# A fused attention, gated layer and SoLU layer on one core: the last pair's end on GpSimd, four raw buffers, new tables of due times and dummy transposes

## The chip, the cores and the metric

The kernel runs on one core of a Trainium2 chip. The metric is the device time of one execution in microseconds (us). The core's engines work side by side, each through its own queue in order: TensorE (PE, matmuls and transposes), VectorE (DVE), ScalarE (ACT), GpSimd (POOL) and SyncE (SP, which here only issues DMAs). They wait for one another by semaphores.

## The reference

Three layers in a row, all in float32 with 64-bit weights (float64 in the inputs):

```python
# 1. attention: 4 batches, 8 heads, 576 tokens, 64 per head, q and k rotated
scores = 1 / sqrt(64) * rotate(q) @ rotate(k).T
attn = exp(scores - max(scores)); attn /= sum(attn) + 1e-9
x = (attn @ v) -> [2304 tokens, 512]
# 2. gated layer, 512 -> 1536 -> 512
x = (sigmoid(x @ w_gate) * (x @ w_val)) @ w_out
# 3. SoLU layer, 512 -> 1024 -> 512
h = x @ w_in; s = h * softmax(h)
out = (((s - mean) / sqrt(var + 1e-6)) * g_ln) @ w_out
```

## The kernel before, in words

**Precision.** Each float32 operand of a matmul is split into a high part in float32r (an ACT or DVE copy) and a low part (a subtraction on DVE or POOL), and three products are added. So around every matmul there are copies and subtractions on the other engines.

**Attention** runs 16 pairs of heads (`i`, `NPR` = 16; pair `i` is batch `i // 4`, heads `2 * (i % 4)` and the next). A pair has nine score tiles (`order`, `NTL` = 9). For each tile PE makes the scores (`scores`), DVE the row maximum, ACT the exponentials, PE four transposes of them (`transpose_e`, "te"), ACT and DVE the two halves of the transposed tile ("et"), and PE the products with v (`attend`, "av"). POOL rotates q and k of the next pair (`turn`), and PE, ACT and DVE turn those into the stacked operands (`qk_bank`, "bank"). For the first pair this is done by hand: `turn_first` rotates in four parts on DVE and POOL, `qk_bank(0, part)` transposes into three PSUM banks, and 20 small copies and subtractions (`job_first`, `stack_first`, named `first.head.step.n`) fill the operands; the scores of head 0 need those of head 0. At a pair's end two joins (DMA) bring the halves of two heads together, two adds and one scale write x in SBUF (`add`, `scale_x`: on POOL, for the last pair on DVE), and `x_out` writes x to memory, from SP. Around the end of this layer the first unit of the gated layer is already computed (`plain`), from x of the first blocks (`x_plain`), and the first weights are decoded (`job_early`).

**Order in attention.** Every step is a job with an engine, what it reads and writes, and a due time from the table `NEED`: a key such as `te.5.2` (step te, tile 5, third job) gives a time, to which 16.83 us (`PERIOD`) times the pair is added; `@0`, `@15` override it for one pair. `emit_attention` sorts the jobs by due time and each engine gets its own in that order. The times that jobs carry there (`took`) and `gate` do not enter it.

**The gated layer** runs three groups of weights (`s`) over three blocks of 768 tokens (`b`), each with four units of products (7 products by Strassen's scheme, only the very first block plainly) and two outputs. The weights come as 64-bit words: SP loads a raw tile, ACT makes the magnitude (`w_mag`, into `mag`), DVE joins sign, magnitude and low bits (`w_sign`, `w_or_mag`, `w_or_low`); this is `decode`, and it has two raw and two magnitude buffers in turn. `split_x` splits x of a block, `keep_p` and `keep_i` decode the weights of the third layer in between and put them by in memory. `KEEP_I` says from which time of which block.

**The SoLU layer** runs nine pairs of token tiles (`job_h`, `job_n`, `job_p`, `job_u`, `job_j`).

**Order in the later layers.** `run_jobs` plans them: a list scheduler with assumed durations that gives each engine, when it is free, the ready job with the lowest due time. Here the due times are written in the code, as `need - 5` and the like. SP's queue holds first the DMAs of attention and then those of this plan.

The change touches `qk_bank` (212), `x_out` (363), the first banks (669), `job_scores` (723), `turned_out` (742), `job_add` (783), `job_scale` (804), `job_x_out` (809), `NEED` (1027), `decode` (1204) and `KEEP_I` (1316).

Of the kernel before, what the change touches and what calls it, by code (L numbers as in the profile page):

```python
# [20 lines left out]
def kernel(  # L21
# [21 lines left out]
    nc = tc.nc  # L43
# [168 lines left out]
    def qk_bank(i, part):  # L212

        raw = turned[i].rearrange("p i h d -> p i (h d)")
        if part == 0:
            stacks[i, 0] = st_t[i % 2][0]
            stacks[i, 1] = st_t[i % 2][1]
# [145 lines left out]
    def x_out(hp, bl, c, n):  # L363
        nc.sync.dma_start(out=xd[bl][hp, :, c - bl * BT:c - bl * BT + n], in_=x_sb[hp][:, c:c + n])
# [284 lines left out]
    if True:  # L649
# [72 lines left out]

    def job_scores(g):
        i, n = divmod(g, NTL)
        begin("scores", i, n)
        reads = []
        for h in (0, 1) if order[n] is None else (order[n][0],):
            reads += row_stacks(i, h, 0, 3)
        if order[n] is None:
            reads.append(one(f"qtl{i % 2}", 0, 2))  # L730
        took = (1.06 if order[n] is None else 0.53) * (2.0 if g < 4 else 1.0)
        writes = [one(f"S{g % 2}")] + ([one(f"sum{i % 4}", 0, NTL)] if n == 0 else [])
        ajob(nc.tensor, took, lambda: found.__setitem__(("s", g), scores(i, n)), reads, writes)
# [33 lines left out]
    def job_attend(i, h, j, m0, m1):  # L767
# [4 lines left out]
        if m1 == 9:  # L772
            e = (A, V)[SLOTS["uw"][2 * h + j]]
            ajob(e, 0.365 if e is V else 0.3, lambda: high(e, *found["av"][0][1:]), (one("AV"),), (one(uw, *c),))
# [8 lines left out]
    def job_add(i, h):  # L783
        e = (G, V)[i == NPR - 1]
        ajob(e, 1.42 if e is G else 0.67, lambda: add(i, h, e), (one(f"uw{(2 * i + h) % 4}", 0, S), one(f"um{i % 2}", h, h + 1)), (x_rows(i, h),), True)
# [10 lines left out]
    def job_weigh_out(i):  # L796
        ajob(V, 0.2, lambda: weigh_out(i, 0), (found.pop(("tr", i)),), (one("rt"),))
# [6 lines left out]
    def job_scale(i):  # L804
        e = (G, V)[i == NPR - 1]
        x = [x_rows(i, h) for h in range(2)]
        ajob(e, 1.42 if e is G else 0.67, lambda: scale_x(i, e), [one(f"wt{i % 2}", 0, 3)] + x, x, True)

    def job_x_out(i):
        b, hp = pairs[i]  # L810
        c = b * S
        while c < (b + 1) * S:
            bl = c // BT
            n = min((bl + 1) * BT, (b + 1) * S) - c
            ajob(SP, n * 0.5 * KB, lambda bl=bl, c=c, n=n: x_out(hp, bl, c, n), [x_rows(i, h) for h in range(2)], (one(f"xd{bl}", hp, hp + 1),))
# [34 lines left out]
    def job_stack_left(i):  # L850
        for h in range(2):
            ajob(G, 0.2, lambda h=h: stack_left(i, h), row_stacks(i, h, 1, 2, "l"), (one(f"qtl{i % 2}", h, h + 1),))
# [107 lines left out]
    for m, t in enumerate((7.9, 10.0, 10.25)):  # L960
# [60 lines left out]
    for m in chunks:  # L1021
# [939 lines left out]
```

## Time and profile before

| | |
|---|---|
| median of 3 runs | 915.3 us (914.73 to 915.69) |
| profiled execution | 915.11 us, its span 913.2 us |
| busy, share of the span | PE 97%, DVE 89%, ACT 72%, POOL 37% |
| TensorE's mean granted clock | 0.997 of full |
| DMA | 147.33 MB, mean 161 GB/s |

The span runs from the first to the last instruction of the profiled execution. A busy time is the time in which an engine had an instruction at work; matmuls overlap, and their ends are modelled. A line number is that of the kernel. A releaser is what ended an engine's wait.

### The profile page before, as it was taken

To read this page: it belongs to the slowest core of one execution; us is meant where nothing else is said; L and a number is where in the kernel's file an instruction comes from. 1 tells how busy PE (TensorE), PEld (TensorE's weight loads), DVE (VectorE), ACT (ScalarE), POOL (GpSimd) and SP (SyncE) were. 2 spreads that over 40 slices of the span, in tenths; PEclk is the share of its full clock that TensorE was granted. 3 is DMA by queue.
4 is the path that set the end of the run, shared out by engine and by line. 5 is a ranking of instruction groups with operands and counts; after the bars stand their busy time and mean duration, and the time that the engine had idled before them with its cause. 6 is when DMAs were issued, how large, how long until landed. Compare 5 with 4: busy or idle time off the path is not lost.

```text
span 913.2 us, 16106 instructions
## 1 busy us (share of the span) xinstructions
PE 882.9 (97%) x5354; PEld 833.1 (91%) x5354; DVE 810.2 (89%) x1523; ACT 653.5 (72%) x1379; POOL 339.3 (37%) x296
## 2 busy tenths in 40 slices
PE   4999999999999999999999999999999999999998
PEld 3999999999998999999999999999999877888886
DVE  5999999999997798999998999999987499999971
ACT  4999999999995465666667666666565276777751
POOL 7679899898845000011011121212030243233200
PEclk9999999999999999999999999999999999999999
DMA  4667777678663762425275864659599834454332
GB/s 127 159 183 196 205 200 197 184 209 214 155 165 112 221 216 81 151 81 196 86 230 135 260 133 145 129 174 229 179 250 364 185 124 93 99 109 81 81 70 46
DMA packets 120882, 147.33 MB, mean 161 GB/s; under 512 B 44752, under 2 KB 90080, under 8 KB 120800
## 3 DMA queue, kind: packets, MB, share of 16 engines
q1 hardware_dynamic: 113888, 136.87, 51.4%
q0 software_dynamic: 6912, 9.44, 7.1%
q8 instruction: 42, 0.69, 0.3%
q14 instruction: 40, 0.33, 0.1%
HBM read 77.76 MB, written 37.30 MB: 126 GB/s over the span
## 4 chain that ended last, share of the span: by engine, by line
PE 73%; DVE 19%; issue 3%; DMA 2%; ACT 2%; POOL 0%; SPq 0%; DVEq 0%; ACTq 0%
PE s L291 9%; PE av L420 8%; PE te L379 7%; DVE xs L544 2%; PE tq L222 2%; PE far_c L1869 2%; PE far_b L1869 2%; PE far_c L1871 2%; PE far_b L1870 2%; PE far_c L1870 2%; PE far_b L1871 2%; PE tk L400 1%; DVE w L469 1%; PE near_a L630 1%; PE near_a L629 1%
## 5 line engine op out<-in xcount | busy, mean ns | idle before, releaser
L298 DVE TENSOR_REDUCE nm<-s 128x1 f32<-128x576 f32 x144 | 108.2, 752 | 11.5 <-PE s L291 9.0
L303 ACT ACTIVATE e<-s,nm 128x576 f32<-128x576 f32 x144 | 107.7, 748 | 7.4 <-DVE nm L298 6.0
L291 PE MATMUL s<-st 128*128 128x288 f32 x512 | 96.6, 312 | 5.5 <-DVE st L251 3.9
L373 DVE TENSOR_TENSOR et<-te,et 128x512 fp32r<-128x512 f32 x144 | 95.8, 676 | 1.4 <-ACT et L370 1.3
L420 PE MATMUL av<-et,vs 128*128 128x288 f32 x512 | 94.4, 312 | 0.4 <-POOL vs L202 0.4
L1457 POOL DMA_DIRECT2D yd<-yst x40 | 36.0, 1280 | 141.1 <-ACT yst L486 141.1
L370 ACT CAST et<-te 128x512 fp32r<-128x512 f32 x144 | 81.2, 587 | 7.8 <-PE te L379 6.4
L379 PE MATMUL te<-ident,e 128*128 128x128 f32 x576 | 81.9, 274 | 2.5 <-DVE et L373 2.4
L291 PEld LDWEIGHTS s<-st 128*128 128x128 f32 x512 | 75.1, 193 | 6.8 <-ACT st L249 4.2
L420 PEld LDWEIGHTS av<-et,vs 128*128 128x128 f32 x512 | 73.3, 191 | 0.7 <-POOL vs L202 0.6
L379 PEld LDWEIGHTS te<-ident,e 128*128 128x128 f32 x576 | 67.4, 141 | 5.1 <-DVE et L373 2.5
L540 ACT CAST xs<-xst 128x384 fp32r<-128x384 f32 x110 | 50.7, 518 | 13.7 <-DVE xst L535 11.5
L544 DVE TENSOR_TENSOR xs<-xst,xs 128x384 fp32r<-128x384 f32 x112 | 56.4, 548 | 2.2 <-ACT xs L540 2.0
L1538 POOL TENSOR_TENSOR xs<-xst,xs 128x512 fp32r<-128x512 f32 (+1 forms) x14 | 17.5, 1254 | 72.7 <-ACT xs L1535 72.7
L431 POOL TENSOR_TENSOR x_sb<-uw,um 64x576 f32<-64x576 f32 x30 | 43.2, 1439 | 2.5 <-DMA um<-uw 0.4
L494 POOL TENSOR_TENSOR wv<-w,wv 128x512 fp32r<-128x512 f32 (+1 forms) x3 | 5.2, 1743 | 103.3 <-ACT wv L486 103.3
L170 POOL TENSOR_TENSOR turned_t<-raw_t,other_t 128x576 f32<-128x576 f32 (+1 forms) x30 | 40.5, 1369 | 1.2
L463 ACT ACTIVATE mag<-raw_w 128x512 f32<-128x512 f32 x52 | 34.9, 676 | 7.9 <-DMA raw_w<-in_moe_w_val_dram 3.7
L162 POOL TENSOR_TENSOR other_t<-raw_t,rope_sb 128x1152 f32<-128x1152 f32 x14 | 37.4, 2674 | 5.6 <-DMA raw_t<-in_q_dram 4.5
L162 POOL TENSOR_TENSOR raw_t<-raw_t,rope_sb 128x1152 f32<-128x1152 f32 x14 | 37.3, 2664 | 1.1
L1811 POOL TENSOR_TENSOR st<-st,mhalf 128x1 f32<-128x1 f32 x18 | 15.9, 884 | 54.9 <-DVE st L1810 53.7
L629 PE MATMUL near_a<-xs,wg 128*128 128x384 f32 x96 | 32.3, 337 | 2.1 <-ACT held L1363 2.1
(475 smaller groups left out, 3068.4 us busy)
## 6 DMA issues: line engine op xcount, KB each, us to landing
st<-st SPq DMA_DIRECT2D x45, 288.0 KB, 4.0
xst<-xd SPq DMA_DIRECT2D x32, 384.0 KB, 6.0
raw_w<-in_moe_w_out_dram SPq DMA_DIRECT2D x20, 512.0 KB, 4.5
yd<-yst POOLq DMA_DIRECT2D x40, 192.0 KB, 6.5
st<-st SPq DMA_DIRECT2D x47, 144.0 KB, 2.4
raw_w<-in_moe_w_gate_dram SPq DMA_DIRECT2D x12, 512.0 KB, 4.3
raw_w<-in_moe_w_val_dram SPq DMA_DIRECT2D x12, 512.0 KB, 3.7
cd<-mag SPq DMA_DIRECT2D x22, 256.0 KB, 5.5
```

What stands on the lines that cost most here:

```text
L162: eng.tensor_mul(out=(o, x)[step], in0=x, in1=w.to_broadcast([P, n, 2, D // 2]))
L291: nc.tensor.matmul(ps[:, j, :HALF], w, x, start=m == 0, stop=m == len(mm) - 1)
L298: nc.vector.tensor_reduce(out=nm, in_=ps[:, :, :HALF], axis=AX.XY, op=ALU.max, negate=True)
L303: nc.scalar.activation(out=e.rearrange("p (j c) -> p j c", j=2), in_=ps[:, :, :HALF], func=AF.Exp, bias=nm, accum_out=sums[i][:, n:n + 1],)
L370: nc.scalar.copy(out=h_out, in_=ps)
L373: nc.vector.tensor_sub(out=l_out, in0=ps, in1=h_out.bitcast(F32))
L379: nc.tensor.transpose(ps[:, r * P:(r + 1) * P], e[:, r * P:(r + 1) * P], ident)
L420: nc.tensor.matmul(av[:, :HALF], *mm[m], start=m == 0, stop=m == len(mm) - 1)
L431: eng.tensor_add(out=x_sb[hp][rows, b * S:(b + 1) * S], in0=uws.pop((i, h))[rows], in1=uws[i][rows])
L540: nc.scalar.copy(out=t[:, 0], in_=here)
L544: l_eng.tensor_sub(out=t[:, 1], in0=here, in1=t[:, 0].bitcast(F32))
L629: nc.tensor.matmul(out, wh, t[:, 0], start=fresh and j == 0, stop=False, skip_group_check=not fresh)
```

## The change

1. **The last pair's end.** `job_add` and `job_scale` use POOL for all pairs. The last pair's `x_out` is issued from POOL's queue; for the others it stays on SP.
2. **Raw buffers.** The first six decodes of the gated layer use four raw and four magnitude buffers in the order 0, 2, 3, 1, 0, 2 (magnitudes 0, 2, 3, 1, 0, 2); the two new ones of each kind lie in the tiles yst and xst, which have no other use yet.
3. **The attention table.** All 446 entries of `NEED` have new values (below, a few of them set together).
4. **Dummy transposes.** `keep_clock(n)` issues n transposes of the identity into a PSUM tile that nobody reads: 30 before the first banks, 16 behind them, and 5, 5 and 4 behind the scores of tiles 1, 2 and 3 of the first pair.
5. **Shifts.** In the later layers each job gets a name (`place`), and a table `SHIFT` of 800 entries adds a number of us to the due times of the jobs that it names. `KEEP_I` starts the two jobs 6 and 5 us earlier. Some assumed durations differ, of which only that of `w_sign` (0.34 to 0.36) reaches the planner of the later layers.

```diff
-    def x_out(hp, bl, c, n):
-        nc.sync.dma_start(out=xd[bl][hp, :, c - bl * BT:c - bl * BT + n], in_=x_sb[hp][:, c:c + n])
+    def x_out(hp, bl, c, n, eng):
+        eng.dma_start(out=xd[bl][hp, :, c - bl * BT:c - bl * BT + n], in_=x_sb[hp][:, c:c + n])
...
+        idle_ps = ps_av.tile([P, 512], F32, tag="av", name="idle")
+
+        def keep_clock(n):
+            for _ in range(n):
+                nc.tensor.transpose(idle_ps[:, 0:P], ident, ident)
+
+        keep_clock(30)
         first.extend(qk_bank(0, part)[0][2] for part in range(3))
-        pass
+        keep_clock(16)
...
+    IDLE_AFTER = {1: 5, 2: 5, 3: 4}
...
+        def run():
+            found["s", g] = scores(i, n)
+            if i == 0 and n in IDLE_AFTER:
+                keep_clock(IDLE_AFTER[n])
...
     def job_add(i, h):
-        e = (G, V)[i == NPR - 1]
-        ajob(e, 1.42 if e is G else 0.67, lambda: add(i, h, e), ...)
+        ajob(G, 1.42, lambda: add(i, h, G), ...)
...
     def job_scale(i):
-        e = (G, V)[i == NPR - 1]
...
+            e = (SP, G)[i == NPR - 1]
+            ajob(e, n * 0.5 * KB if e is SP else 1.3, lambda bl=bl, c=c, n=n, e=e: x_out(hp, bl, c, n, e), ...)
...
     NEED = {
-        "first.0.0.0": -33.81, "first.0.0.1": -62.21, "first.1.0.0": -47.43,
+        "first.0.0.0": -320.064, "first.0.0.1": -167.555, "first.1.0.0": -241.355,
...
-        "te.4.2@15": 32.63, "softmax.8.0@15": 35.64, "add.0.0@15": 65.1,
+        "te.4.2@15": 39.745, "softmax.8.0@15": 49.04, "add.0.0@15": 91.357,
...
-        "early.3.v.1.1536.3": 292.64, "early.3.v.1.1536.4": 294.63, "x_plain.B22.1.1": 262.71, "plain.7.0": 326.42,
+        "early.3.v.1.1536.3": 285.916, "early.3.v.1.1536.4": 288.006, "x_plain.B22.1.1": 380.509, "plain.7.0": 481.022,
...
+    plain_job, names_of = job, []
+    SHIFT = { ... }
+    def job(eng, took, fn, reads=(), writes=(), need=0.0, port=None):
+        key = f"{step[0]}.{step[2]}"
+        step[2] += 1
+        names_of.append(key)
+        plain_job(eng, took, fn, reads, writes, need + SHIFT.get(key, 0.0), port)
...
+    RAWS = [(raw_w[n], one(f"raw{n}")) for n in range(2)]
+    RAWS += [(yst_t[:, 1024 * n:1024 * n + 1024].bitcast(I64), one("yst", 1024 * n, 1024 * n + 1024)) for n in range(2)]
+    MAGS = [(mags[n], one(f"mag{n}")) for n in range(2)]
+    MAGS += [(xst_t[:, 2048 + 512 * n:2560 + 512 * n], one("xst", 2048 + 512 * n, 2560 + 512 * n)) for n in range(2)]
+    AHEAD = [(RAWS[r], MAGS[m]) for r, m in ((0, 0), (2, 2), (3, 3), (1, 1), (0, 0), (2, 2))]
...
-    KEEP_I = {(2, 0): (0, 36.0), (2, 1): (1, 25.0)}
+    KEEP_I = {(2, 0): (0, 30.0), (2, 1): (1, 20.0)}
```

## Rows read from the trace of the kernel before

**Rows 1.** The page's head and its part 1, busy us of each engine.

```profile
span 913.2 us, 16106 instructions
PE 882.9 (97%) x5354; PEld 833.1 (91%) x5354; DVE 810.2 (89%) x1523; ACT 653.5 (72%) x1379; POOL 339.3 (37%) x296
```

**Rows 2.** Stages: length; busy us (xinstructions) PE, PEld, DVE, ACT, POOL; PEclk; DMA; GB/s.

```profile
0.00:40.00 40.00, 25.80 (x157) 23.16 (x158) 28.83 (x59) 26.69 (x63) 25.23 (x26) 1.00 0.53 137
16.00:26.00 10.00, 9.25 (x48) 8.87 (x47) 5.83 (x10) 6.29 (x16) 9.84 (x8) 1.00 0.42 109
40.00:60.00 20.00, 20.00 (x161) 19.31 (x160) 19.10 (x34) 18.70 (x45) 16.93 (x13) 1.00 0.76 198
280.00:300.00 20.00, 17.80 (x117) 17.23 (x116) 13.70 (x21) 7.55 (x17) 7.38 (x7) 1.00 0.39 126
300.00:340.00 40.00, 38.00 (x213) 36.47 (x212) 35.43 (x67) 24.13 (x48) 0.74 (x1) 1.00 0.71 232
420.00:700.00 280.00, 276.12 (x1576) 274.04 (x1575) 262.38 (x511) 185.61 (x398) 44.90 (x47) 0.99 0.65 186
580.00:584.00 4.00, 4.00 (x16) 4.00 (x15) 3.83 (x9) 1.81 (x4) 2.14 (x3) 0.57 1.09 145
720.00:780.00 60.00, 57.21 (x266) 46.69 (x265) 55.43 (x116) 41.12 (x72) 18.00 (x19) 1.00 0.41 104
```

**Rows 3.** PE's waits by releaser: us in total, times, longest us.

```profile
PE te L379 <- DVE et L373: 2.4, 2, 2.2
PE near_a L629 <- ACT held L1363: 2.1, 2, 2.0
...
PE far_d L645 <- DVE wv L494: 0.7, 1, 0.7
```

**Rows 4.** The chain that ended last, at two places: start us, us, what.

```profile
15.69 1.10 PE s L291 x3
...
19.82 0.85 PE tq L222 x4
20.67 0.96 PE s L291 x4
...
56.03 1.15 PE s L291 x8
57.18 0.87 PE te L379 x8
```

**Rows 5.** The first 18 us: start us, us, engine, line, what [idle before <-releaser].

```profile
1.00 0.29 POOL masks.py:199 TENSOR_SCALAR_AFFINE_SELECT ident<-ident 128x128 f32<-128x128 f32 x1
...
6.89 1.09 PE L222 MATMUL tq<-ident,turned_t 128*128 128x128 f32 x4 [6.89 <-DVE turned_t L170]
...
10.14 1.40 ACT L249 CAST st<-tq 64x512 fp32r<-64x512 f32 x3 [4.61 <-PE tq L222]
...
12.07 0.58 ACT L249 CAST st<-tq 64x512 fp32r<-64x512 f32 x1 [0.53 <-DVE st L251]
...
15.42 2.76 POOL L170 TENSOR_TENSOR turned_t<-w,other_t 128x576 f32<-128x576 f32 x2
```

**Rows 6.** DVE and POOL in time near the end of attention.

```profile
282.96 1.49 POOL L431 TENSOR_TENSOR x_sb<-uw,um 64x576 f32<-64x576 f32 x1
283.20 1.80 DVE L469 SCALAR_TENSOR_TENSOR w<-mag,w 128x512 int32<-128x512 int32 x1
...
300.88 0.69 DVE L469 SCALAR_TENSOR_TENSOR w<-mag,w 128x512 int32<-128x512 int32 x1 [0.34 <-ACT mag L463]
...
303.29 0.76 DVE L351 TENSOR_TENSOR x_sb<-x_sb,wt 128x576 f32<-128x576 f32 x1
```

**Rows 7.** SP's DMA issues in time, same stretch.

```profile
298.68 0.54 SPq L426 DMA_DIRECT2D um<-uw  x1
304.07 0.33 SPq L364 DMA_DIRECT2D xd<-x_sb  x1
304.50 1.01 SPq L456 DMA_DIRECT2D raw_w<-in_moe_w_val_dram  x2
```

More of the change, by code (lines that the diff above doesn't have):

```diff
@@ L214, in qk_bank @@
         raw = turned[i].rearrange("p i h d -> p i (h d)")
-        if part == 0:
-            stacks[i, 0] = st_t[i % 2][0]
-            stacks[i, 1] = st_t[i % 2][1]
+        stacks[i, 0], stacks[i, 1] = st_t[i % 2]
         st = stacks[i, 0]
@@ L730, in job_scores @@
             reads.append(one(f"qtl{i % 2}", 0, 2))
-        took = (1.06 if order[n] is None else 0.53) * (2.0 if g < 4 else 1.0)
+        took = 1.06 if order[n] is None else 0.53
+        if i == 0 and n in IDLE_AFTER:
+            took += 0.11 * IDLE_AFTER[n]
         writes = [one(f"S{g % 2}")] + ([one(f"sum{i % 4}", 0, NTL)] if n == 0 else [])
-        ajob(nc.tensor, took, lambda: found.__setitem__(("s", g), scores(i, n)), reads, writes)
+        def run():
+            found["s", g] = scores(i, n)
+            if i == 0 and n in IDLE_AFTER:
+                keep_clock(IDLE_AFTER[n])
+        ajob(nc.tensor, took, run, reads, writes)
     def job_softmax(g):
@@ L773, in job_attend @@
             e = (A, V)[SLOTS["uw"][2 * h + j]]
-            ajob(e, 0.365 if e is V else 0.3, lambda: high(e, *found["av"][0][1:]), (one("AV"),), (one(uw, *c),))
+            ajob(e, 0.365 if e is V else 0.39, lambda: high(e, *found["av"][0][1:]), (one("AV"),), (one(uw, *c),))
     def job_join(i, h):
@@ L783, in job_add @@
     def job_add(i, h):
-        e = (G, V)[i == NPR - 1]
-        ajob(e, 1.42 if e is G else 0.67, lambda: add(i, h, e), (one(f"uw{(2 * i + h) % 4}", 0, S), one(f"um{i % 2}", h, h + 1)), (x_rows(i, h),), True)
+        ajob(G, 1.42, lambda: add(i, h, G), (one(f"uw{(2 * i + h) % 4}", 0, S), one(f"um{i % 2}", h, h + 1)), (x_rows(i, h),), True)
     def job_weigh(i):
@@ L796, in job_weigh_out @@
     def job_weigh_out(i):
-        ajob(V, 0.2, lambda: weigh_out(i, 0), (found.pop(("tr", i)),), (one("rt"),))
+        ajob(V, 0.27, lambda: weigh_out(i, 0), (found.pop(("tr", i)),), (one("rt"),))
         ajob(SP, 0.2, lambda: weigh_out(i, 1), (one("rt"),), (one(f"d{i % 2}"),))
@@ L804, in job_scale @@
     def job_scale(i):
-        e = (G, V)[i == NPR - 1]
         x = [x_rows(i, h) for h in range(2)]
-        ajob(e, 1.42 if e is G else 0.67, lambda: scale_x(i, e), [one(f"wt{i % 2}", 0, 3)] + x, x, True)
+        ajob(G, 1.42, lambda: scale_x(i, G), [one(f"wt{i % 2}", 0, 3)] + x, x, True)
     def job_x_out(i):
@@ L814, in job_x_out @@
             n = min((bl + 1) * BT, (b + 1) * S) - c
-            ajob(SP, n * 0.5 * KB, lambda bl=bl, c=c, n=n: x_out(hp, bl, c, n), [x_rows(i, h) for h in range(2)], (one(f"xd{bl}", hp, hp + 1),))
+            e = (SP, G)[i == NPR - 1]
+            ajob(e, n * 0.5 * KB if e is SP else 1.3, lambda bl=bl, c=c, n=n, e=e: x_out(hp, bl, c, n, e), [x_rows(i, h) for h in range(2)], (one(f"xd{bl}", hp, hp + 1),))
             c += n
@@ L834, in job_split_v @@
         raw, hi, lo = one(f"rawv{i % 2}", 0, 3), one(f"vs{i % 2}", 0, 1), one(f"vs{i % 2}", 1, 2)
+        if i == 0:
+            gate[len(jobs)] = 10.8
         ajob(A, 0.63, lambda: split_v(i, 0), (raw,), (hi, lo, one("order_vs")))
@@ L851, in job_stack_left @@
         for h in range(2):
-            ajob(G, 0.2, lambda h=h: stack_left(i, h), row_stacks(i, h, 1, 2, "l"), (one(f"qtl{i % 2}", h, h + 1),))
+            ajob(G, 0.25, lambda h=h: stack_left(i, h), row_stacks(i, h, 1, 2, "l"), (one(f"qtl{i % 2}", h, h + 1),))
     first_t = []
@@ L959 @@
     begin("turned", None)
-    for m, t in enumerate((7.9, 10.0, 10.25)):
+    for m, t in enumerate((7.5, 9.7, 9.85)):
         gate[len(jobs)] = t
@@ L1179, with place @@
     jobs, seen, gate = [], {}, {}
+    plain_job, names_of = job, []
+    SHIFT = {
[133 rows of a table added]
+    }
+    def place(*name):
+        step[:] = [".".join(map(str, name)), None, 0]
+    def job(eng, took, fn, reads=(), writes=(), need=0.0, port=None):
[3 more added lines that the diff above has]
+        plain_job(eng, took, fn, reads, writes, need + SHIFT.get(key, 0.0), port)
     def xs_at(name, j):
@@ L1202 @@
     raws_used = [0]
+    RAWS = [(raw_w[n], one(f"raw{n}")) for n in range(2)]
[3 more added lines that the diff above has]
+    AHEAD = [(RAWS[r], MAGS[m]) for r, m in ((0, 0), (2, 2), (3, 3), (1, 1), (0, 0), (2, 2))]
     def decode(kind, n, dst, dst_at, need):
         k = raws_used[0] % 2
+        (raw, r), (mag, m) = (AHEAD[raws_used[0]:] or [((raw_w[k], one(f"raw{k}")), (mags[k], one(f"mag{k}")))])[0]
         raws_used[0] += 1
-        raw, mag, dst = raw_w[k], mags[k], dst.bitcast(I32)
-        r, m = one(f"raw{k}"), one(f"mag{k}")
+        dst = dst.bitcast(I32)
         job(SP, 1.7, lambda: w_load(kind, n, raw), (), (r,), need - 8)
         job(A, 0.57, lambda: w_mag(raw, mag), (r,), (m,), need - 5)
-        job(V, 0.34, lambda: w_sign(raw, dst), (r,), (dst_at,), need - 5, True)
+        job(V, 0.36, lambda: w_sign(raw, dst), (r,), (dst_at,), need - 5, True)
         job(V, 0.6, lambda: w_or_mag(mag, dst), (m, dst_at), (dst_at,), need - 4, True)
@@ L1230, in make_pair @@
     def make_pair(s, n, need):
+        place("pair", s, n)
         for j in range(2):
@@ L1238, in make_plain @@
     def make_plain(n, need):
+        place("plain", n)
         of, done = 1024 * (n % 2), (2, 2, 2, 0)[n]
@@ L1315 @@
     KEEP = {(1, 1): range(0, 5), (1, 2): range(5, 8)}
-    KEEP_I = {(2, 0): (0, 36.0), (2, 1): (1, 25.0)}
+    KEEP_I = {(2, 0): (0, 30.0), (2, 1): (1, 20.0)}
     def make_unit(kind, n, where, need):
+        place("w", kind, n)
         k = raws_used[0] % 2
@@ L1328, in load_x @@
     def load_x(b, need):
+        place("x", *now, b)
         for kk in range(KD):
@@ L1425, in output @@
     def output(s, b, half, setn):
+        place("out", s, b, half)
         bank, need = banks[setn], out_at(s, b, half)
@@ L1463 @@
     END = unit_at(*LAST, 4) + 2 * OUT
+    now = [0]
     for s in range(NF // FG):
+        now[:] = [s]
         if s:
@@ L1669, in job_turn_ln @@
         hi_w, lo_w = LT_AT[t % 2]
+        had = list(step)
+        place("turn", t)
         for n in range(2):
@@ L1675, in job_turn_ln @@
             job(V, 0.6, lambda n=n: turned_ln(t, n, 1), (at_, hi), (lo,), need + n + 1, False)
+        step[:] = had
     def job_j(t, need):
+        place("j", t)
         at_ = one("bank", 5 + t % 2, 6 + t % 2)
```

19 lines of the change are left out of this document (15 added, 4 removed), and 320 rows, old and new, of tables (NEED, SHIFT).

## The prediction, made before the result was known

> **What bounds the kernel now.** First the page's head and its busy line: TensorE (PE) is busy 882.9 of the 913.2 us span [rows 1]. PE's own work sets the time, and a change that keeps every real matmul can win only PE's idle time, about 30 us, and what PE loses at its lower clock. The profiled execution took 915.11 us, 1.9 more than its span, and the median of the three runs (915.3) lies 0.2 above it, so I add 2.1 to a forecast span.
>
> Next the busy time by stage, to see where those 30 us lie [rows 2]. From 40 to 60 us PE never idles (161 instructions in 20 us, 0.124 us each); the attention layer up to 280 us is like that but for less than 1 us, and nothing that is reordered there can pay. The first 40 us hold 157 instructions, worth 19.5 us: 20.5 are lost, 14.2 of them idle and 6.3 because PE runs slowly. Then 2.20 us idle in 280 to 300, 2.00 in 300 to 340, 3.88 in 420 to 700, 2.79 in 720 to 780. In 580 to 584 the granted clock was 0.57 of full, which loses 0.43 x 4 = 1.7 us. The reader is to see that VectorE (DVE) is nearly as full as PE in the late stages: 262.4 of 280, 17.6 free, and 3.83 of 4 at 580.
>
> Then the list of PE's waits, for what comes last [rows 3]: DVE's evacuation ahead of a transpose (2.4 in all), ScalarE's (ACT) "held" copy (2.1), DVE's wv half (0.7). In each an in-order engine did something less urgent first, which is what a table of due times can mend.
>
> **The change part by part.** *Start: the order.* ACT's first copy begins at 10.14 and had waited 4.61 us [rows 5], since the old table puts `first.0.0.1` (due -62, second bank) ahead of `first.0.0.0` (-34); the first bank's transposes start at 6.89 and take about 1.1 [rows 5]. The new table has `first.0.0.0` lowest, so one copy of 0.58 us goes into that hole, and the two halves that the first scores need no longer stand behind head 1's. Against that, two engines that read one bank go one after the other (the copy at 12.07 waited 0.53 for DVE [rows 5]), and head 1's copy of the first bank now stands behind a DVE instruction. Before, the scores got going at 15.69 [rows 4]. ACT's copies saved ahead of that point are two of 0.58 and one of 0.21, 1.4 us, if nothing else is late; the idle of 0.53 and about 0.6 more could go with them. I take 1.2, ends 0 and 2.3.
>
> *Start: the clock.* 30 dummy transposes before the first real ones, 16 behind them, 14 behind scores 1 to 3. Four transposes took 0.85 at 19.82 and eight took 0.87 at 57.18; four score matmuls took 0.96 at 20.67 and eight 1.15 at 56.03 [rows 4]: 0.212 against 0.109 and 0.240 against 0.144, so PE was on the lower of its two levels (1.2 of 2.4 GHz) until about 24 us (by the same chain). From 15.69 to there it ran some 19 score matmuls and 13 transposes: 19 x 0.096 + 13 x 0.103 = 3.2 us that a warm clock gives back. It cannot all arrive: pair 1's banks wait for GpSimd's (POOL) rotation, which ends at 15.42 + 2.76 = 18.18 [rows 5], and ACT and DVE are busy 6.29 and 5.83 of the 10 us from 16 to 26 [rows 2], so they have 3.7 and 4.2 to catch up with. I take 1.3, 40% of 3.2. The dummies' own cost: the 30 need 30 x 0.212 = 6.4 us at the low level, from 1.3, when POOL has written the identity, to 7.7 [rows 5]; they hold up only the bank due at 6.89, by 0.8 at most, inside ACT's hole of 4.61 us. The 16 take 3.4 even at 0.212 and lie between the last bank and the scores. The 14 stand in PE's queue ahead of the next scores: at 0.109 1.5 us, in waits for exponentials that are there anyway; at 0.212 3.0 us, of which perhaps half shows, 1.5. So the clock part lies between +1.5 and -3.2. Start in all: -2.5, ends +1.5 and -5.5.
>
> The Trainium skill ("TensorE: Matmul & The Clock Gate", Part 4, PE-mode transpose) says that transposes in that mode do not count as activity and do not bring the full clock. No row here shows transposes alone before a rise: in the stretch ahead of this one transposes and score matmuls alternate. It is a rival below.
>
> *End of attention.* The last pair's two adds and its scale leave DVE (0.76 us each, 2.3 in all [rows 6]) for POOL (1.49 for an add, which I take for the scale too [rows 6]). POOL is idle there in 300 to 340 (0.74 busy [rows 2]), so its longer time is hidden, and the x it makes (block 2) is loaded only after block 1. But DVE pays when POOL works beside it: a decode step took 1.80 at 283.20, with POOL adding from 282.96, against 0.69 at 300.88 [rows 6]. With 3 x 1.49 = 4.5 us of POOL, and 1.1 lost in each 1.5, DVE would lose up to 3.3 and save 2.3: from 2.3 better to 1.0 worse. The output DMA goes to POOL's queue: SP issued it only at 304.07, after the scale at 303.29 had run, and the two weight loads queued behind it went out at 304.50 [rows 6, 7]. Now SP passes: what is left ahead of the loads is the last join, so up to 5 us earlier; the join went out at 298.68 [rows 7]. With four raw buffers, two of them in yst and xst, four loads can be in flight instead of two; but those lie where the et tiles were, free only after the last attends (about 296), which is no later than the loads. So the wv halves that PE waited for (0.7 [rows 3] and the rest of the 2.00 us in 300 to 340) should be on time. The 2.20 us before that are a transpose behind DVE's early decode of three slow steps; the new table sets the last two steps ahead of `te.4.2` and the softmax maximum of tile 8 behind them. It moves the collision rather than removes it; I give it half. New on POOL: the last `x_plain` (B22) now stands behind the last pair's first add, which waits for a DMA; PE's `plain.7` needs it. If late, it costs up to 1 us. Sum: -1.6 (of 2.0), -1.1 (of 2.2), +0.2 for the new wait: -2.5, ends +2.0 (1.0 more DVE time and 1 for the wait) and -4.2.
>
> *Later layers.* The shifts change no operation, only which ready job an engine takes first. They can win at most 3.88 + 2.79 + 1.7 = 8.4 us [rows 2]; the 1.7 goes with the 2 us wait for ACT's "held" [rows 3] that precedes it. I take -3.5, four tenths: the waits are of the kind that a table mends, but DVE has one part in 16 free, and eight hundred shifts also move jobs that were in time. Ends +5 and -8.4. The upper end is DVE's: the two weight-keeping jobs start 6 and 5 us earlier in a stretch where DVE is 3.83 of 4 busy [rows 2]; 5 is the smaller of the two moves.
>
> Sum: 913.2 - 2.5 - 2.5 - 3.5 = 904.7, plus 2.1 = 906.8 us.
>
> **Rivals.** *The dummies leave the clock low.* For it: the clock rose only near 24 us though PE had transposed from 6.89 on; against: 2.8 of the 7.4 us of work before the rise (13 x 0.212 and 19 x 0.240) was transposes. Then 1.2 won, 1.5 lost, the rest as forecast: 913.2 + 0.3 - 2.5 - 3.5 + 2.1 = 909.6. By the rule of that page of the Trainium skill this is the case that comes.
>
> *The shifts are worth nothing on the chip*: every wait removed comes back elsewhere, as DVE has no more than 17.6 us free in the 280 from 420 to 700 [rows 2]. The shifts' size and sign, up to 118 us both ways, speak neither for nor against. 913.2 - 2.5 - 2.5 + 2.1 = 910.3.
>
> *Nothing but the start moves*: POOL's work slows DVE as much as it relieves it, PE waits for the same decode, the shifts give nothing. 913.2 - 1.2 + 2.1 = 914.1.
>
> *Slower: the keeping jobs collide.* Place: 560 to 640. With due times 6 and 5 us lower, their decode and halves go ahead of PE's own splits and "held" sums on a DVE that is full. Price: up to 6 + 5 = 11 us of PE waits, with a low clock after a long one (1.7 as at 580) inside it. At 8 us lost, with start and attention end won: 913.2 - 5.0 + 8 + 2.1 = 918.3. It decides once PE waits over 5 us more there than now. Against it: a job with a later due time yields, and PE's own splits have earlier ones.
>
> **How the numbers follow.** Chances: forecast 0.52, clock low 0.15, shifts worthless 0.15, only the start 0.09, collision 0.09. What a measurement of this kernel can tell from no change is about 0.2%, 1.8 us: faster is below 913.5, slower above 917.1. Forecast and the first two rivals fall below 913.5 but for a few hundredths, the fourth case mostly between, the collision above: faster 0.82, same 0.09, slower 0.09. The forecast's own ends are 899 (two terms near their best) and 912; the range reaches on to "only the start": 900.5 to 914.5.
>
> **What would show it.** Right: eight transposes near 0.9 us and scores of eight near 1.15 before 20 us; the first scores at or before 14.5; weight loads behind the last join before 302 and no PE wait on wv; under 1 us of PE idle in 300 to 340 and under 6 in 420 to 780; no stretch of low clock at 580. Wrong: transposes of four still near 0.85 at the start of the scores; new PE waits on POOL's xs; DVE decode steps of 1.8 us in the attention end; PE idle above 7 us in 420 to 780.

## The result, and the profile after

The changed kernel takes 906.4 us (median of 904.35 to 908.41) where the kernel before takes 915.09: a ratio of 0.9904, interval 0.9881 to 0.9928. In a second set of runs (experiment 1) it took 904.65, ratio 0.9885 (0.9871 to 0.9898). 906.8 was forecast, in a range of 900.5 to 914.5.

The busy line of the changed kernel, in its slowest execution (908.41 us, span 906.6), against [rows 1]:

```profile
PE 886.6 (98%) x5414; PEld 838.6 (92%) x5414; DVE 801.7 (88%) x1517; ACT 660.2 (73%) x1388; POOL 340.8 (38%) x294
```

The 60 new PE instructions are the dummies. The stages of the same execution, columns as in [rows 2], with two stretches more (120 to 280 and 400 to 420):

```profile
0.00:40.00 40.00, 32.87 (x240) 30.34 (x241) 31.56 (x63) 29.14 (x68) 29.32 (x28) 1.00 0.60 152
120.00:280.00 160.00, 157.35 (x1241) 151.52 (x1239) 154.15 (x261) 151.56 (x361) 134.41 (x105) 1.00 0.72 186
280.00:300.00 20.00, 18.57 (x110) 18.48 (x111) 13.82 (x23) 10.50 (x23) 7.00 (x8) 0.91 0.50 156
300.00:340.00 40.00, 39.59 (x229) 39.18 (x228) 34.01 (x67) 22.53 (x49) 3.79 (x3) 1.00 0.64 224
400.00:420.00 20.00, 19.04 (x110) 18.72 (x110) 19.66 (x39) 12.30 (x26) 3.88 (x3) 1.00 0.38 132
420.00:700.00 280.00, 278.73 (x1595) 275.81 (x1594) 260.04 (x512) 188.20 (x402) 42.03 (x45) 1.00 0.68 193
580.00:584.00 4.00, 4.00 (x24) 3.74 (x23) 3.96 (x8) 2.67 (x8) 0.00 (x0) 1.00 0.81 194
720.00:780.00 60.00, 58.34 (x272) 47.86 (x271) 55.43 (x121) 44.85 (x77) 22.63 (x23) 1.00 0.36 106
```

Read it against [rows 2] as a ledger of PE's idle time and granted clock. Start: 240 less 60 dummies is 180 matmuls in 40 us, 23 more than before; at 0.124 us each, 2.9 us won. 120 to 280: the kernel before was busy 159.26 of the 160 us, so it idled 0.74, now 2.65: 1.9 lost. 280 to 300: idle falls from 2.20 to 1.43, but the granted clock is 0.91, which is 1.8 us. 300 to 340: idle from 2.00 to 0.41. 400 to 420: 0.96 idle is new. 420 to 700: from 3.88 to 1.27, and the low clock at 580 is gone (0.57 to 1.00). 720 to 780: from 2.79 to 1.66. Together 2.9 - 1.9 + 0.8 - 1.8 + 1.6 - 1.0 + 2.6 + 1.7 + 1.1 = 6.0 of the 6.6 us between the spans.

That ledger is rough, since the same stretch of time holds different work in the two kernels, and PE can count as busy while its matmuls lie further apart. A second one counts matmuls. Here are the first 400 us of the kernel before, of this execution and of a second one that was profiled (experiment 1, span 902.5); at 400 us PE is in the gated layer in all three, with a matmul every 0.171 us (117 in 20 us):

```profile
0.00:400.00 400.00, 380.86 (x2717) 366.70 (x2718) 361.47 (x652) 323.26 (x753) 236.44 (x190) 1.00 0.62 173
```
```profile
0.00:400.00 400.00, 388.38 (x2795) 376.84 (x2796) 364.56 (x657) 328.17 (x757) 244.79 (x194) 1.00 0.64 174
```
```profile
0.00:400.00 400.00, 391.21 (x2819) 380.45 (x2820) 366.11 (x665) 330.44 (x763) 247.08 (x195) 1.00 0.64 174
```

Less the 60 dummies, the first execution is 18 matmuls ahead of the kernel before at 400 us, 3.1 us, and the second 42, 7.2 us. With the first 40 us (23 and 20 ahead, at 0.124) and the spans (913.2, 906.6, 902.5), that gives, in us won:

| part | forecast | first execution | second execution |
|---|---|---|---|
| first 40 us | 2.5 | 2.9 | 2.5 |
| rest of attention and first units, to 400 us | 2.5 | 0.2 | 4.7 |
| behind 400 us | 3.5 | 3.5 | 3.5 |
| span | 8.5 | 6.6 | 10.7 |

So the two executions differ almost only between 40 and 400 us. In the second, the end of attention shows no low clock and no idle at all:

```profile
0.00:40.00 40.00, 33.70 (x237) 30.99 (x238) 31.25 (x63) 28.88 (x68) 29.48 (x28) 0.96 0.60 149
280.00:300.00 20.00, 20.00 (x128) 19.95 (x127) 13.70 (x23) 10.82 (x22) 8.22 (x8) 1.00 0.62 194
300.00:340.00 40.00, 40.00 (x232) 39.74 (x231) 36.18 (x72) 23.76 (x50) 0.92 (x2) 1.00 0.63 223
```

A wait of 1.9 us lies at the start of this stretch or just ahead of it in both; a low clock of 3.4 us followed it in the first alone.

PE in time at the start of the changed kernel (start us, us, engine, line, what [idle before <-releaser]), against [rows 4, 5]:

```profile
1.34 5.38 PE L671 MATMUL idle<-ident 128*128 128x128 f32 x30 [1.34 <-POOL ident masks.py:199]
6.74 0.66 PE L220 MATMUL tq<-ident,turned_t 128*128 128x128 f32 x4
...
13.73 1.54 PE L289 MATMUL s<-st 128*128 128x288 f32 x8 [1.85 <-DVE st L249]
```

Four transposes take 0.66 at 6.74, against 1.09 [rows 5]: nothing but transposes ran before. By the rule of the Trainium skill ("TensorE: Matmul & The Clock Gate", Part 4, PE-mode transpose) the clock would have stayed low; the trace does not agree, though it records these transposes as MATMUL and does not say whether they run in the mode that the page means. The rise lies inside the 30, in the first six us by pieces of two:

```profile
0.00:2.00 2.00, 0.66 (x3) 0.66 (x4) 0.60 (x3) 1.28 (x1) 0.68 (x6) 1.00 0.04 10
2.00:4.00 2.00, 2.00 (x12) 2.00 (x11) 0.07 (x1) 0.15 (x1) 0.00 (x0) 1.00 0.85 263
4.00:6.00 2.00, 2.00 (x14) 2.00 (x13) 1.97 (x6) 1.48 (x6) 0.59 (x1) 1.00 0.77 209
```

The first three take 0.22 us each, as at the lower of the two levels (1.2 GHz); 14 in two us is 0.14 on the way to the upper (2.4); the 16 dummies at 9.97 took 1.91, 0.12 each.

### The profile page after: what moved, and what is told of

It reads as the page before. It is cut to its first block, busy times and chain, and to the rows that moved or that the text cites. A ratio compares the mean times of both kernels' runs of the same rounds, so it can differ in the third digit from the quotient of the medians.

```text
span 906.6 us, 16253 instructions
## 1 busy us (share of the span) xinstructions
PE 886.6 (98%) x5414; PEld 838.6 (92%) x5414; DVE 801.7 (88%) x1517; ACT 660.2 (73%) x1388; POOL 340.8 (38%) x294
## 4 chain that ended last, share of the span: by engine, by line
PE 67%; DVE 20%; issue 4%; ACT 3%; DMA 3%; POOL 2%; SPq 1%; DVEq 0%; ACTq 0%; POOLq 0%
PE s L289 7%; PE av L418 7%; PE te L377 6%; DVE xs L542 3%; PE far_b L2065 2%; PE far_b L2066 2%; PE far_c L2066 2%; PE far_c L2067 2%; PE far_b L2067 2%; PE far_c L2065 2%; DVE xst L533 2%; PE tq L220 1%; DVE gs L1569 1%; PE tk L398 1%; PE far_a L627 1%
## 5 line engine op out<-in xcount | busy, mean ns | idle before, releaser
L296 DVE TENSOR_REDUCE nm<-s 128x1 f32<-128x576 f32 x144 | 106.3, 746 | 8.3 <-PE s L289 7.4
L377 PE MATMUL te<-ident,e 128*128 128x128 f32 x576 | 84.6, 274 | 2.2 <-DVE et L371 1.9
L289 PEld LDWEIGHTS s<-st 128*128 128x128 f32 x512 | 73.1, 189 | 4.7 <-DVE st L249 2.1
L429 POOL TENSOR_TENSOR x_sb<-uw,um 64x576 f32<-64x576 f32 x32 | 47.9, 1495 | 15.3 <-DMA um<-uw 13.2
L1725 POOL TENSOR_TENSOR xs<-xst,xs 128x512 fp32r<-128x512 f32 (+1 forms) x13 | 15.5, 1199 | 64.5 <-ACT xs L1722 61.8
L533 DVE TENSOR_TENSOR xst<-xst 128x384 f32<-128x384 f32 x64 | 34.6, 553 | 0.7
```

The source lines that it names most:

```text
L289: nc.tensor.matmul(ps[:, j, :HALF], w, x, start=m == 0, stop=m == len(mm) - 1)
L296: nc.vector.tensor_reduce(out=nm, in_=ps[:, :, :HALF], axis=AX.XY, op=ALU.max, negate=True)
L377: nc.tensor.transpose(ps[:, r * P:(r + 1) * P], e[:, r * P:(r + 1) * P], ident)
L429: eng.tensor_add(out=x_sb[hp][rows, b * S:(b + 1) * S], in0=uws.pop((i, h))[rows], in1=uws[i][rows])
L533: t_eng.tensor_sub(out=here, in0=x, in1=y)
```

## The experiments

All times stand beside the kernel before on the same chip in the same set; a difference between two changed kernels is judged by the two ratios' intervals. Differences in us are of medians; a ratio weighs all runs, so the two can differ where the times of one kernel fall into two groups.

**1. The changed kernel itself**, unchanged.

> The changed kernel itself, so that the others have it on the same chip. 906.4 us, with single times from 904 to 909. Theory A: the spread of 4 us (the kernel before has 1) is the low clock of 3.4 us near 282, which comes in some executions and not in others and costs about 1.7; then an execution without it is near 904.3. Rival B: the spread comes from transfers that land early or late, and the low clock lies there in every execution.

904.65 us, 0.9885 (0.9871 to 0.9898). The profiled execution, 904.24, has the full clock near 282, as theory A says, but another low stretch in the first 40 us (mean 0.96); so the place of a low clock changes. It does not make the spread by itself: the executions with a mean granted clock of 1.000, so without any low stretch, took 906.04 (first set) and 905.06, and 904.35 and 904.24 came with 0.998.

**2. No dummies.**

```diff
-            for _ in range(n):
+            for _ in range(0 * n):
```

> The changed kernel without any of the 60 dummy transposes; all else stays. Theory A (the prediction's term, 1.3 us): without them the four transposes of a bank take about 0.85 again and the first scores run at the low level of the clock until some 8 us after they began; about 1.3 us slower, 907.7, with ends 906.4 and 909.4. Rival B (dummies do not raise the clock, the new order alone made the start shorter): 906.4 or less, since 1.5 us of dummies between the scores go.

906.79, 0.9910 (0.9895 to 0.9925): 2.1 more than with them, the intervals just touching. Its first 40 us, the stretch from 300 to 340, and the first scores, then those of the kernel before:

```profile
0.00:40.00 40.00, 26.66 (x166) 24.52 (x167) 30.04 (x61) 27.61 (x65) 28.06 (x27) 1.00 0.56 143
300.00:340.00 40.00, 38.64 (x221) 38.01 (x221) 34.42 (x66) 22.26 (x47) 3.52 (x3) 1.00 0.63 220
```
```profile
13.81 2.38 PE L289 MATMUL s<-st 128*128 128x288 f32 x8 [3.45 <-DVE st L249]
```
```profile
14.24 0.58 PE L291 MATMUL s<-st 128*128 128x288 f32 x1 [3.90 <-DVE st L251]
15.69 2.05 PE L291 MATMUL s<-st 128*128 128x288 f32 x7 [0.87 <-ACT st L256]
```

In the kernel before the first score started at 14.24, and 15.69 [rows 4] is the start of the other seven. By the order alone the eight are done at 16.19 instead of 17.74, but they take 2.38 against 1.54 with the dummies. 166 matmuls against 157 [rows 2] are the order's share, 9 x 0.124 = 1.1 us; 180 against 166 the dummies', 14 x 0.124 = 1.7 (177 and 1.4 in the second execution of the changed kernel). The rest of the 2.1 us does not lie at the start: from 300 to 340 this run idles 1.36 us, 1.0 of it a wait for a wv half, which the second execution does not have.

**3. The kernel before with the dummies.**

```diff
+        keep_clock(30)
         first.extend(qk_bank(0, part)[0][2] for part in range(3))
-        pass
+        keep_clock(16)
...
+            found["s", g] = scores(i, n)
+            if i == 0 and n in IDLE_AFTER:
+                keep_clock(IDLE_AFTER[n])
```

> The kernel before with the 60 dummy transposes at the same places (30, 16, and 5, 5, 4 behind scores 1 to 3) and its own table. Theory A: the clock is up at 6.9 us and the scores run at 1.15 for eight; but ACT's hole of 4.6 us ahead of its first copy stays, so that less than half of it arrives: 914 us, 1 less than before. Rival B: the whole 3.2 us of low clock comes back without the new order: 912. Rival C: the dummies lie in the way of the scores: 915.5 to 916.5.

913.33, 0.9985 (0.9974 to 0.9996): 2.1 less than before by the medians, 1.4 (0.4 to 2.4) by the ratio, since six of its eleven times lie from 912.47 to 913.33 and five from 915.00 to 916.60. Its first 40 us hold 173 real matmuls, 16 more than before: 2.0 us. The size lies between A and B. The dummies need no new order to pay.

**4. No shifts, keeping jobs at the old places.**

```diff
-        plain_job(eng, took, fn, reads, writes, need + SHIFT.get(key, 0.0), port)
+        plain_job(eng, took, fn, reads, writes, need, port)
...
-    KEEP_I = {(2, 0): (0, 30.0), (2, 1): (1, 20.0)}
+    KEEP_I = {(2, 0): (0, 36.0), (2, 1): (1, 25.0)}
```

> The changed kernel with all shifts of the later layers at nothing and the two keeping jobs at their old places (36 and 25). Theory A: the shifts gave what the idle time of PE says, 2.6 us between 420 and 700, 1.1 between 720 and 780 and 1.7 of low clock near 580: 906.4 + 5.4 = 911.8, with the low clock back between 560 and 640. Rival B: the later layers are better because they start from another point in time and order, not by the shifts: 907, and PE idles under 4 us in 420 to 780 without them.

909.96, 0.9947 (0.9934 to 0.9960): 5.3 more, the intervals clear of each other. Its later layers:

```profile
400.00:420.00 20.00, 20.00 (x117) 20.00 (x116) 19.59 (x39) 12.13 (x26) 2.61 (x3) 1.00 0.43 138
420.00:700.00 280.00, 276.68 (x1582) 273.47 (x1581) 260.70 (x512) 183.55 (x394) 44.20 (x47) 1.00 0.67 191
720.00:780.00 60.00, 55.23 (x250) 44.76 (x249) 54.20 (x116) 42.15 (x71) 17.45 (x20) 0.97 0.36 101
```

3.32 us idle in 420 to 700 (1.27 with the shifts), 4.77 in 720 to 780 (1.66), and 1.8 us of low clock there: 2.1 + 3.1 + 1.8 = 7.0, less the 0.96 that the shifts cost at 400, in an execution of 912.0. Theory A in kind; the low clock came at 720 to 780, not near 580. By count this execution is 33 matmuls (5.6 us) ahead of the kernel before at 400 us and keeps 3.0 to the end: without the shifts its later layers are 2.6 us slower than in the kernel before. So 5.3 is what the shifts are worth to the changed kernel; what its later layers gain on the kernel before is 3.5. Why the old due times do worse here than there stays open.

**5. The shifts off, the keeping jobs at their new places** (the second edit of experiment 4 left out).

> The changed kernel with all shifts at nothing, but the two keeping jobs at their new places (30 and 20). Against it stands the kernel with neither, 909.96. Theory A: the keeping jobs' move is worth nothing by itself, the shifts did it: 910.0. Rival B (the prediction's slower case, in small): 6 and 5 us earlier without the shifts they collide with PE's own splits: 912 to 915, and PE idles over 4 us between 560 and 640. Rival C: the move did it all: 905.

911.91, 0.9957 (0.9943 to 0.9972), not told apart from experiment 4. PE idles 3.67 us in 560 to 640 against 2.21 there, and 0.9 in the changed kernel: without the shifts the move does no good; what it does with them, no run shows. A third reading, C, is out.

**6. The old due times for the middle pairs.** The keys without `@` take them: pairs 2 to 14, and most jobs of pair 1, for which the table has few keys of its own. A job that can go goes when the order stands still.

```diff
-        "add.0.0": 45.067, ...
+        "add.0.0": 42.42, ...
...
+                for n in [x for x in queue if not jobs[x][3] - done][:1 if stuck and e is not None else None] if e is None or stuck else queue[:1]:
```

> The changed kernel with the due times of the middle pairs (2 to 14 of the attention layer) from the old table; the new ones for pairs 0, 1 and 15 and for jobs without a pair stay. Where the sorted order would stand still, the next job that can go goes. Theory A: the new table costs the middle of the attention layer 1.9 us of PE idle between 120 and 280 (POOL's scale late for the next pair's rotation, DVE's halves late for a transpose), which the old times did not have; 904.65 - 1.9 = 902.8 on this chip, with under 1 us of idle there. Rival B: those waits only move what the end would wait for anyway, or the two tables do not fit together at the seams: 904.5 to 906.

943.54, 1.0317 (1.0304 to 1.0330): rival B, at a price that neither theory had. From 40 to 60 us PE is busy 9.48 of 20, with 53 matmuls against 162 in the changed kernel, 13.5 of the 39 us; the chain of waits, in time, shows why:

```profile
37.90 2.17 DMA raw_t<-in_q_dram
...
45.58 2.73 POOL turned_t L170 x2
```

The load went out at 37.90, in the changed kernel at 31.61, and POOL's rotation ends at 48.3 against 42.7; SP had issued the pair before it 6 us late already (22.41 against 16.35). The two tables do not fit at the seams, and the run says nothing on the 1.9 us in the middle. Where the other 25 us go was not followed.

**7. The whole old table**, with the second edit of experiment 6.

```diff
-        "add.0.0@15": 91.357, ...
+        "add.0.0@15": 65.1, ...
```

> The changed kernel with the whole old table of the attention layer (dummies, POOL's last pair, four raw buffers, shifts and keeping jobs as changed; where the sorted order would stand still, the next job that can go goes). Theory A: the new table's worth is the start's order (1.1 us by the matmuls of the first 40 us without dummies) and the attention end (1.6 + 0.8), less 1.9 in the middle: 904.65 + 1.6 = 906.3. Rival B: the shifts were made for the new table's order, and without it the later layers fall back too: 910 or more.

914.54, 0.9992 (0.9984 to 1.0001). B's number, but not its reason: 9.9 more than the changed kernel, yet the later layers keep the shifts' gain (278.76 busy of 280 in 420 to 700). The loss is at the end of attention. POOL, DVE and PE there, in time, and the clock of 296 to 300:

```profile
291.62 1.39 POOL L429 TENSOR_TENSOR x_sb<-uw,um 64x576 f32<-64x576 f32 x1 [7.42 <-DMA um<-uw]
...
294.04 0.25 POOL L314 TENSOR_SCALAR sum<-sum 128x9 f32<-128x9 f32 x1
```
```profile
294.33 0.22 DVE L316 RECIPROCAL sum<-sum 128x9 f32<-128x9 f32 x1 [5.00 <-POOL sum L314]
```
```profile
294.69 0.27 PE L321 MATMUL tr<-ident,sum 128*9 128x128 f32 x1 [2.65 <-DVE sum L316]
```
```profile
296.00:300.00 4.00, 4.00 (x18) 4.00 (x17) 2.69 (x5) 0.41 (x1) 0.00 (x0) 0.59 0.07 13
```

The reader is to follow it upwards: PE's transpose waits for DVE's reciprocal, that for POOL's short sum, and the sum stands in POOL's queue behind the last pair's first add, which waits 7.42 us for a DMA. In the new table the sum stands ahead of that add (283.77 against 288.41 in the changed kernel).

**8. The last pair's end on DVE and SP again**, with the new table.

```diff
-        ajob(G, 1.42, lambda: add(i, h, G), ...
+        e = (G, V)[i == NPR - 1]
+        ajob(e, 1.42 if e is G else 0.67, lambda: add(i, h, e), ...
...
-            e = (SP, G)[i == NPR - 1]
+            e = SP
```

> The changed kernel with the last pair's two adds and its scale on DVE again and its output DMA on SP; all else stays. Theory A (the prediction's step): SP issues the weight loads behind that DMA again, up to 5 us later, DVE spends 2.3 us more at the end of the attention layer, and PE waits for a weight half in 300 to 340: 906.1, 1.5 more than the changed kernel. Rival B: the four raw buffers have the loads in flight already, and nothing is late: 904.7. Rival C: DVE is better off without POOL beside it: 904.

904.19, 0.9884 (0.9870 to 0.9898): the same time. SP's issues there, against [rows 7], DVE's scale ahead of them, and SP's first load in the changed kernel:

```profile
296.67 0.33 SPq L362 DMA_DIRECT2D xd<-x_sb  x1
297.04 0.43 SPq L454 DMA_DIRECT2D raw_w<-in_moe_w_val_dram  x1
```
```profile
295.88 0.76 DVE L349 TENSOR_TENSOR x_sb<-x_sb,wt 128x576 f32<-128x576 f32 x1
```
```profile
298.53 0.39 SPq L454 DMA_DIRECT2D raw_w<-in_moe_w_val_dram  x1
```

The loads go out as early with the output DMA ahead of them: the new table has the last add and scale done by 296.6 on DVE. In the kernel before the scale began at 303.29 [rows 6], and that, not the queue, had held SP until 304.07 [rows 7]. Rival B has the time; its reason, buffers already in flight, is not what the rows show.

**9. The old table with the end on DVE and SP**, both edits.

> The changed kernel with the whole old table and the last pair's adds, scale and output DMA at their old places (DVE and SP); dummies, four raw buffers, shifts and keeping jobs as changed. With the last pair's end on POOL and the old table it took 914.5. Theory A: the old table doesn't fit an end on POOL; PE waits 2.6 us for the sums' reciprocal, which stood behind POOL's add, and 3.4 us of low clock lie there: with the end on DVE both go, and the dummies (2.1) and shifts (5.3) are left: 915.3 - 7.4 = 907.9. Rival B: the old table doesn't fit the four raw buffers: 914.

908.29, 0.9929 (0.9916 to 0.9942): theory A. POOL's end costs 6.2 us with the old table and nothing with the new one; the new table is worth 4.1 with the end on DVE and 9.9 with it on POOL. Its 280 to 300:

```profile
280.00:300.00 20.00, 17.79 (x103) 17.29 (x102) 12.07 (x18) 7.15 (x16) 5.26 (x5) 0.91 0.42 136
```

2.21 idle, against 4.85 in experiment 7, and a mean clock of 0.91 against 0.83: the wait for the sum (2.65) and the low clock behind it (0.41 x 4 = 1.6) are most of the 4.8 us between the two spans.

**10. Two raw buffers.**

```diff
-    AHEAD = [(RAWS[r], MAGS[m]) for r, m in ((0, 0), (2, 2), (3, 3), (1, 1), (0, 0), (2, 2))]
+    AHEAD = []
```

> The changed kernel with two raw weight buffers instead of four; all else stays. Theory A: with two loads in flight instead of four, the decode of the weights for the first units is late, and PE waits in 300 to 340 as before, 1 to 2 us: 906.2. Rival B: the loads go out behind the last join anyway, and DVE's decode sets the pace: 904.7. Rival C: a load that waits for a buffer stands at the head of SP's queue, and the loads of x behind it are late: 908.

909.14, 0.9932 (0.9919 to 0.9945): 4.5 more than with four, but PE does not idle in 300 to 340 (40.00 of 40). Of theory A's place nothing is seen; 420 to 700 has 2.78 idle against 1.27. By count it is 29 matmuls (5.0 us) ahead of the kernel before at 400 us and 5.9 at the end: behind 400 us it wins 0.9, where the changed kernel wins 3.5.

**11. Two raw buffers and no shifts** (experiments 4 and 10 together).

> The changed kernel with two raw buffers, no shifts and the keeping jobs at their old places. Against it stands the same with four raw buffers, 909.96. Taking the two extra buffers from the changed kernel cost 4.5 us. Theory A: four buffers are worth that by themselves, loads being in flight earlier: 914.5. Rival B: most of the 4.5 came because the shifts are fitted to the order that four buffers give, and miss with two: 910 to 911.5.

912.48, 0.9966 (0.9952 to 0.9979), against 909.96 with four: 2.5 more, the intervals overlap. In the profiled executions the count speaks for B: at 400 us it is 45 matmuls (7.7 us) ahead of the kernel before, and 4.8 are left at the end, so 2.9 are lost behind 400 us, against 2.6 in experiment 4 with four buffers. So there two buffers in place of four cost 2.6 us behind 400 us with the shifts and 0.3 without: the shifts fit the order that four buffers give.

**12. One due time moved.** In the changed kernel DVE's slow decode step lies ahead of an evacuation that PE waits for 1.9 us, and a hole of 1.74 us follows; here it moves into the hole.

```diff
-        "early.3.v.1.1536.4": 288.006,
+        "early.3.v.1.1536.4": 307.3,
```

> The changed kernel with one due time moved: the last step of the early decode (early.3, step 4) from 288.0 to 307.3, so that it stands behind two evacuations of te, ahead of which it ran 1.79 us with POOL beside it. Theory A: PE's wait for that evacuation, 1.9 us in the changed kernel, goes, and the step fits into DVE's own hole of 1.74 us a little later: 904.65 - 1.9 = 902.8, and no low clock follows, since in the changed kernel's first profile it followed this wait. Rival B: the step is late for the weight halves instead, or PE waits for the next evacuation: 904.65.

903.33, 0.9872 (0.9858 to 0.9887): 1.3 less than the changed kernel's, in intervals that overlap. The trace is plainer than the time. POOL's instruction beside the step and DVE in time, in the changed kernel's second execution and here, and the stages here:

```profile
276.40 1.73 POOL L429 TENSOR_TENSOR x_sb<-uw,um 64x576 f32<-64x576 f32 x1 [0.95 <-DMA um<-uw]
```
```profile
276.89 1.79 DVE L472 SCALAR_TENSOR_TENSOR w<-raw_w,w 128x512 int32<-128x512 int32 x1
278.60 0.68 DVE L371 TENSOR_TENSOR et<-te,et 128x512 fp32r<-128x512 f32 x1
...
283.08 1.29 DVE L371 TENSOR_TENSOR et<-te,et 128x512 fp32r<-128x512 f32 x2 [1.74 <-ACT et L368]
```
```profile
277.95 1.42 POOL L349 TENSOR_TENSOR x_sb<-x_sb,wt 128x576 f32<-128x576 f32 x1 [0.64 <-DMA wt<-d]
```
```profile
276.09 0.69 DVE L371 TENSOR_TENSOR et<-te,et 128x512 fp32r<-128x512 f32 x1
...
278.77 1.15 DVE L472 SCALAR_TENSOR_TENSOR w<-raw_w,w 128x512 int32<-128x512 int32 x1
```
```profile
120.00:280.00 160.00, 159.70 (x1266) 154.65 (x1265) 153.82 (x266) 153.82 (x367) 136.02 (x107) 1.00 0.71 186
280.00:300.00 20.00, 20.00 (x123) 19.95 (x122) 14.37 (x24) 10.25 (x21) 9.00 (x8) 1.00 0.73 234
```

PE's wait is gone: 0.30 us of idle from 120 to 300, against 2.50 in the changed kernel's second execution, less 0.41 that is new from 300 to 340. The median is the lowest of all, and the span, 900.8, is 1.7 below that of the second execution; that it is faster than the changed kernel is not shown by the times.

The step's time follows from POOL: it ends 0.55 us after the POOL instruction that was running when it began, at 278.68 after 278.13, and here at 279.92 after 279.37; in the kernel before, at 285.00 after 284.45 [rows 6].

## Why the prediction was right

*Start, order, -1.2:* 1.1 by the matmuls of the first 40 us (experiment 2). Right. Its mark, first scores by 14.5, says nothing, though it was met with 13.73: the kernel before had its first score at 14.24. The row at 15.69 that the prediction took for it is the start of the other seven.

*Start, clock, -1.3:* right, if a little small: 1.4 and 1.7 by the matmuls in the two executions, 2.0 in experiment 3, where the ratio gives 1.4 (0.4 to 2.4). The step that gave only 40% of 3.2 us to PE, since ACT and DVE had to catch up, holds: in 16 to 26 us ACT's busy time rose from 6.29 [rows 2] to 7.67 by the order (experiment 2) and to 8.81 with the dummies. The rival of a clock left low falls by the 0.66 us at 6.74.

*The attention middle, nothing:* wrong in one execution. In the second, 2.50 us are idle in 120 to 280, of which 1.89 are the wait of the next step: 0.61 is left, against 0.74 before. In the first, 2.65 are idle and 0.46 of them belong to that wait: 2.19 is left, 1.5 lost. "Nothing that is reordered there can pay" did not ask what can be lost. The longest wait of the first execution there, then POOL and DVE ahead of it, and the same two in the second:

```profile
PE tq L220 <- POOL x_sb L349: 0.8, 1, 0.8
```
```profile
125.05 1.42 POOL L429 TENSOR_TENSOR x_sb<-uw,um 64x576 f32<-64x576 f32 x1
```
```profile
125.30 1.73 DVE L472 SCALAR_TENSOR_TENSOR w<-raw_w,w 128x512 int32<-128x512 int32 x1
```
```profile
125.67 0.67 DVE L472 SCALAR_TENSOR_TENSOR w<-raw_w,w 128x512 int32<-128x512 int32 x1
```
```profile
126.52 1.42 POOL L429 TENSOR_TENSOR x_sb<-uw,um 64x576 f32<-64x576 f32 x1
```

In the first, POOL's add begins 0.25 us ahead of DVE's decode step, and the step takes 1.73; in the second the step comes first and takes 0.67. Among the profiled executions with the new table, the four that have such a slow step between 120 and 235 us (the first one here, experiments 4, 5 and 10) have the wait for x_sb, and the five that have none (experiments 1, 2, 8, 11 and 12) do not. What decides which engine comes first stays open; experiment 6, which was to show the middle, broke elsewhere.

*End of attention, -2.5:* of 4.2 us idle before, 1.9 + 0.41 is left in the first execution, with 1.8 of low clock, and 1.9 in the second: 0.1 and 2.3 won. By count, middle and end together won 0.2 and 4.7; the 2.4 us more in the second lie in part in matmuls that follow one another faster (0.172 us of busy time each in 300 to 340, against 0.178 [rows 2], 1.3 us), and the rest was not followed. So the sum is right for neither execution, and its reasons only in part. The collision of decode and POOL was said to move rather than go, and it did: a step of 1.79 us, one of the prediction's own signs of being wrong, and a PE wait of 1.9 where 2.2 had been [rows 3]; half was credited, 0.3 came, and experiment 12 shows that the rest was to be had. The 1.6 us of 300 to 340 came (1.59 and 2.00). But the reason given, that SP passes the output DMA, carries nothing by experiment 8: it is the due times. And that POOL's longer time is hidden holds only for the new table: with the old one it costs 6.2 us (experiments 7 and 9). The prediction counted the wait that x_plain would get behind POOL's add; the one that decides is the sum's, which it did not look for.

*Later layers, -3.5:* right in size: 3.5 by count in both executions. The idle time and the clock give more, 2.6 + 1.7 + 1.1 - 0.96 = 4.4, with 0.96 at 400 to 420, where PE now waits for a "held" copy on ACT; the matmuls of the same stretches give 3.4 (19 more in 420 to 700 and 6 more in 720 to 780 [rows 2], 110 for 117 in 400 to 420). That the gain is the shifts' is shown by experiment 4. That DVE's full queue would send the waits elsewhere did not come true: it is still busy 260.04 of 280. The two rivals "shifts worthless" and "only the start" fall with it; the collision of the keeping jobs is seen only without shifts and in small (3.67 us idle in 560 to 640).

So the start and the later layers came as forecast, in mechanism and size. That the median of the first set, 906.4, lies 0.4 from 906.8 is luck: between 40 and 400 us, where 2.5 was forecast, single executions won from 0.2 to 4.7, and the second set, at 904.65, lies 2.2 below the forecast.

## What to carry to other kernels

Before work moves to an idle in-order engine, look at what stands behind it in that engine's queue and who waits for that: here the same move cost nothing or 6.2 us, most of it by one short sum. A table of due times belongs to its kernel: its parts' gains do not add, and half of an old table is worse than either. Where one wait is left, its own rows name the instruction to move and the hole it fits. And count an engine's real instructions by a fixed time beside its idle time: here idle time alone mis-sized two of the three parts.

## What the hardware showed that was not expected

Thirty transposes and nothing else brought the full rate: 0.66 us for four, against 1.09. The rows' granted clock does not show this change: it says 1.00 in the first 40 us of the kernel before, where PE ran at half the rate until about 24 us. The trace's list of clock records explains it: it starts only with the rise, at 24.0 us in the kernel before and 23.1 in experiment 2, and at 4.2 to 7.1 us in the twelve profiled executions with dummies (5.3 in the first one here). Ahead of its first record, 1.00 is no reading.

Later in a run the clock falls for stretches of some 3.4 us (longer ones in experiment 6), in which a matmul of 384 columns is recorded with 0.52 us (at 296.28 in experiment 7) instead of 0.33 (at 295.20 there). Those looked at lay behind a PE wait of 1.9 to 2.7 us, but waits of 1.9 and 2.2 passed without one (experiments 1 and 8 at 276, and the kernel before at 285). Seven of the twelve executions with dummies have one at 14 to 20 us; in experiment 1 it follows the wait of 1.9 us for the first scores, and its first 40 us hold 177 real matmuls against 180 without it, 0.4 us.

DVE's decode step and POOL's instruction beside it do not run side by side in these rows: one of the two goes on, and the other ends later. The step takes 0.69 us alone [rows 6] and up to 1.94 behind a POOL add (at 175.63 in the first execution); each slowed step that was looked at ended 0.54 to 0.56 us after POOL's instruction. Where the step goes first it takes 0.68, and the add is recorded with 1.82 instead of 1.42 (at 175.37 and 175.52 in the second execution). DVE's evacuations are not slowed: 0.69 at 276.09 in experiment 12, inside a POOL add from 275.58 to 277.31. Where the two recorded starts lie within some 0.2 us, they do not tell which goes first. What a step loses is then what is left of POOL's instruction when it begins.
